# Attention with a gated second layer: which unit's outputs are turned by TensorE, in a newly searched order of steps

## The chip, the cores and the metric

The kernel runs on one core of one Trainium2 chip. The metric is the device time of one execution in microseconds (us). The engines are named as the profile names them: PE is TensorE, DVE is VectorE, ACT is ScalarE, POOL is GpSimd, SP is SyncE. PE, DVE and ACT compute here; POOL computes small things and issues DMA transfers; SP only issues them.

Executions of the kernel before spread from 169 to 187 us. A run is marked fast up to some 1.5% above the fastest of the same kernel (here up to 171.8 us), and slow above that, mostly with a slightly lower mean TensorE clock. In the rounds of the experiments 44 of its 76 executions were slow. The times run on without a gap at 172 us, so the mark is a convention. There is no other core that could disturb it. I compare fast with fast unless I say otherwise.

## The reference, cut to what matters

```python
# q, k, v: (4 batches, 8 heads, 768 positions, 64)
scores = q @ k.T / 8 - slope[h] * distance        # local window of 96 keys + 8 global keys
a = softmax(scores);  attn = a @ v                # (4, 8, 768, 64)
x = attn.transpose(0, 2, 1, 3).reshape(3072, 512)
h = x @ w_in                                      # (3072, 1024)
solu = h * softmax(h)
ln = (solu - mean) / sqrt(var + 1e-6) * g_ln
out = ln @ w_out                                  # (3072, 512), float32
```

## The kernel before

The work is cut into 12 units (4 batches x 3 stretches of 256 positions), each of two tiles of 128 rows in the second part. The kernel is a list of 662 steps, and the list *is* the schedule: each engine executes its own steps strictly in the order of the list, and waits where a step's input or buffer is not ready. A step that issues a DMA stands in the same list, on the engine that its letter names (S, A or P for SP, ACT or POOL).

```python
ORDER = """
...
M:6:0 o:D:1:0 o:A:1:1 Q:3:1 d:S:0:1 q:P:8:1 gk:2 q:P:10:0 cv:D:5 v:S:6:1 k:S:9:1 S:7:2 X:7:2
...
X:10:2 S:10:1 X:10:1 Q:5:0 O:4:0 A:6:1 E:6:1 o:D:4:0 U:6:1 dq:S:11 eq:D:11 v:P:9:1 cv:D:9 S:9:2
X:9:2 d:S:5:0 L:8 I:8 st:S:2 O:4:1 d:S:6:0 V:8 N:8 Z:P:5:0 S:11:3 S:11:2 X:11:3 Z:P:4:1 gv0:3
...
"""
    queues = {"S": nc.sync, "A": nc.scalar, "P": nc.gpsimd}
    def load_v(queue, u, j):                      # v:P:9:1 = half 1 of unit 9's v, issued by GpSimd
        ...
        queues[queue].dma_start(out=held["v32", u][:, :, j], in_=v[...])      # 256 KB
    def cast_v(engine, u):                        # cv:D:9 on VectorE, cv:A:9 on ScalarE
        t = held["v16", u] = attn.tile([P, H, 2, D], FP16, name="v16", bufs=NV)
        cast(engine, t, held.pop(("v32", u)))
    def pick_global_k(b):                         # gk:2, on GpSimd
        for m in range(2):
            nc.gpsimd.tensor_copy(out=z[rr, :, m * NG : m * NG + NG], in_=kT[rr, :, 0:NG])
    def ff_stats(engine, t):                      # Z:P:u:r: five 128x1 operations on GpSimd
        eng.tensor_scalar(out=w1, in0=s0, scalar1=s0, scalar2=1e-6, ...)
        ... (mean, w2, w3)
        eng.tensor_tensor(out=rs, in0=w3, in1=held["neghalf"], op=ALU.pow)
    def ff_turn(t, h=None):                       # t: turn by TensorE, into a small PSUM buffer
        lT = held["lT", t, h] = small([P, len(cs), P], FP16, "lT")
        for i, c in enumerate(cs):
            nc.tensor.transpose(out=lT[:, i], in_=held["un", t][:, ts(c, P)], ...)
    def ff_turn_dma(queue, t):                    # d: turn by a DMA transpose
        queues[queue].dma_start_transpose(out=held["uT", t, None], in_=held["un", t])
    def warm_up(n, i=0):                          # warm: dummy matmuls on zeros
        t = small([P, 512], FP32, "warm")
        ...
    with tc.manual_schedule():
        for step in ORDER.split():
            run(step)
```

The other letters that the text uses: `A`, `E`, `U`, `Q` are the first matmul of the second part (PE), its exponential (ACT), product (DVE) and square (ACT); `Z` the statistics of a tile (mean and inverse deviation, one column each); `O` the second matmul (PE), `o` its scaling, `st` the store; `S`, `X`, `M`, `L`, `I`, `V`, `N` are scores, exponential, mask, sums, reciprocal, values and norm of the attention; `gS` the scores of the global keys, which need `gk`; `tq` turns (transposes) a unit's q on PE, `dq` and `dk` turn by DMA. PSUM is the memory that PE writes its results to; its "small" buffers are two, its "big" ones three, and a step waits until its buffer is free.

The softmax here doesn't subtract the row's maximum and nothing guards it: scores larger than these inputs give would overflow.

## Time and profile before

| | before |
|---|---|
| time, three runs | 171.25 us median (170.24, 171.25, 177.0) |
| profiled execution | 170.78 us, span 169.0 us, mean clock 1.00 |
| busy share PE / ACT / DVE / POOL | 90% / 83% / 78% / 59% |

The profile sets each engine's busy time beside the span. It is easy to read the 59% of POOL as "room"; the result will turn on that. The prediction shows the stretches it used; three others matter for what follows. Columns: stretch, its length, busy us and instruction count of PE, weight loads, DVE, ACT and POOL, then clock (1.00 is full speed), DMA share and GB/s.

```profile
80.00:90.00 10.00, 8.78 (x92) 4.42 (x90) 9.12 (x13) 8.48 (x16) 9.03 (x17) 1.00 1.09 258
...
120.00:130.00 10.00, 10.00 (x110) 5.36 (x110) 8.91 (x16) 8.45 (x15) 7.51 (x15) 1.00 0.94 196
130.00:140.00 10.00, 10.00 (x122) 5.88 (x118) 6.42 (x8) 8.58 (x13) 3.25 (x10) 1.00 0.36 39
```

PE has a small gap near 80 us and none from 120 to 140, at full clock throughout; POOL is busy 9.03 of 10 us near 80. When POOL issued the two loads of interest, the timeline of POOL shows (start, length, engine, what):

```profile
76.15 0.55 POOL L157 DMA_DIRECT2D q<-in_q_dram  x1
76.69 1.09 POOL L320 COPY kgz<-kT 64x32 f16<-64x32 f16 x2
...
104.05 1.87 POOL L163 DMA_DIRECT2D v<-in_v_dram  x2
```

The first is the second half of unit 8's q, the next the pick of the global keys (`gk:2`), the last contains the second half of unit 9's v, which VectorE casts at 114.22 us: about 9 us after it was issued at some 105.0 (the second of the two in the 1.87 us).

### The profile page before, as it was taken

How to read it: one execution, taken by the hardware profiler on the slowest of the kernel's cores; microseconds unless marked ns; L12 is line 12 of the kernel's file. 1: busy time of each engine (PE TensorE's matmuls, PEld its weight loads, DVE VectorE, ACT ScalarE, POOL GpSimd, SP SyncE). 2: the span in 40 equal slices, each digit the busy share in tenths (PEclk: the TensorE clock that was granted, in tenths of full speed). 3: DMA queues.
4: the chain of work that ended last, by engine and by line, in shares of the span. 5: the costliest groups of instructions: out<-in, count | busy, mean ns of one | idle time of the engine just before them, and what ended most of it. 6: DMA issues, size and time to landing. Idle time of an engine off the chain costs nothing.

```text
span 169.0 us, 3944 instructions
## 1 busy us (share of the span) xinstructions
PE 151.6 (90%) x1487; PEld 81.6 (48%) x1487; DVE 132.0 (78%) x203; ACT 140.0 (83%) x218; POOL 100.3 (59%) x194
## 2 busy tenths in 40 slices
...
GB/s 147 329 349 259 238 238 243 200 376 363 372 258 276 194 170 203 144 245 235 251 292 169 203 312 228 136 215 272 275 77 248 42 2 190 124 186 122 132 181 124
DMA packets 59698, 36.43 MB, mean 215 GB/s; under 512 B 50592, under 2 KB 51104, under 8 KB 59680
## 3 DMA queue, kind: packets, MB, share of 16 engines
...
## 4 chain that ended last, share of the span: by engine, by line
PE 48%; ACT 18%; DMA 14%; POOL 10%; issue 6%; DVE 2%; SPq 1%; DVEq 0%; POOLq 0%; ACTq 0%
PE po L512 17%; PE ph L450 16%; DMA q<-in_q_dram 5%; ACT pt L338 4%; PE lb L398 4%; DMA v<-in_v_dram 4%; ACT e L462 3%; PE warm L230 3%; PE sc L329 2%; ACT sq L475 2%; DMA uT<-un 2%; DMA k<-in_k_dram 2%; PE pa L417 2%; ACT rlb L406 2%; POOL gw L588 2%
## 5 line engine op out<-in xcount | busy, mean ns | idle before, releaser
L512 PE MATMUL po<-gw,uT 128*128 128x512 f16 x192 | 44.8, 380 | 1.4 <-DMA uT<-un 1.1
L450 PE MATMUL ph<-w_in,xT 128*128 128x512 f16 x192 | 44.3, 379 | 1.1 <-DVE xT L435 0.8
L338 ACT ACTIVATE pt<-sc 128x896 f16<-128x896 f32 (+1 forms) x48 | 39.2, 873 | 2.0 <-PE sc L329 1.9
L467 DVE SCALAR_TENSOR_TENSOR un<-e,ph 128x1024 f16<-128x1024 f16 x24 | 29.0, 1218 | 6.4 <-ACT e L462 4.6
L462 ACT ACTIVATE e<-ph 128x1024 f16<-128x1024 f32 x24 | 24.5, 1021 | 7.9 <-PE ph L450 7.6
L450 PEld LDWEIGHTS <-xT 128*128 128x128 f16 x192 | 18.2, 98 | 22.5 <-DVE xT L435 1.5
L512 PEld LDWEIGHTS <-uT 128*128 128x128 f16 x192 | 17.7, 98 | 23.1 <-DMA uT<-un 2.4
L475 ACT ACTIVATE sq<-un 128x1024 f16<-128x1024 f16 x24 | 25.4, 1059 | 2.5 <-DVE un L467 2.0
L345 DVE TENSOR_TENSOR pt<-pt,mask 128x896 f16<-128x896 f16 (+1 forms) x48 | 26.3, 586 | 0.6 <-ACT pt L338 0.6
L488 POOL TENSOR_SCALAR w<-s,w 128x1 f32<-128x1 f32 x24 | 9.9, 414 | 17.7 <-ACT sq L475 15.9
L527 DVE TENSOR_SCALAR osb<-po,rs 128x512 f32<-128x512 f32 x17 | 12.7, 748 | 8.5 <-PE po L512 8.5
L329 PE MATMUL sc<-qT,kT 64*128 64x128 f16 (+2 forms) x256 | 16.6, 248 | 2.8 <-DVE kT L140 1.3
L435 DVE TENSOR_TENSOR xT<-pa,rlb 128x1024 f16<-128x1024 f32 x12 | 14.6, 1220 | 2.5 <-ACT rlb L407 1.8
L490 POOL TENSOR_TENSOR rs<-w,neghalf 128x1 f32<-128x1 f32 x24 | 14.8, 619 | 2.0
L483 POOL TENSOR_SCALAR w<-s 128x1 f32<-128x1 f32 x24 | 14.1, 586 | 2.5 <-ACT e L462 0.4
L140 DVE COPY qT<-qturned 128x1024 f16<-128x1024 f16 x9 | 11.0, 1220 | 5.3 <-PE qturned L301 5.3
L329 PEld LDWEIGHTS <-kT 64*128 64x128 f16 x256 | 9.2, 100 | 10.2 <-issue 6.2
L486 POOL TENSOR_SCALAR w<-mean,w 128x1 f32<-128x1 f32 x24 | 11.6, 483 | 2.4
L407 ACT ACTIVATE rlb<-rlb 128x1024 f32<-128x1024 f32 x12 | 12.7, 1058 | 0.4
L301 PE MATMUL qturned<-ident,q 128*128 128x128 f16 x72 | 6.6, 250 | 7.0 <-POOL hm L242 6.6
L406 ACT ACTIVATE rlb<-lb 128x1024 f32<-128x1024 f32 x12 | 12.3, 1025 | 0.7 <-PE lb L398 0.6
L417 PE MATMUL pa<-pt,v 128*64 128x128 f16 (+2 forms) x256 | 10.9, 232 | 0.0
...
## 6 DMA issues: line engine op xcount, KB each, us to landing
...
```

The costliest lines, as they stand in the source:

```text
L329: nc.tensor.matmul(out=sc[:, m, o : o + e - a], lhsT=held["kT", u - s + j // 2][r, g, ts(j % 2, P)], rhs=qT[r, g, a:e], start=True, stop=True,
L338: nc.scalar.activation(out=pt[:, :, 0:w], in_=held.pop(("sc", u, g))[:, :, 0:w], func=AF.Exp, scale=inv_sqrt_d)
L345: nc.vector.tensor_tensor(out=pt[:, :, 0:w], in0=pt[:, :, 0:w], in1=held["mask"][:, g, :, o : o + w], op=ALU.mult)
L406: nc.scalar.activation(out=rlb, in_=held.pop(("lb", u)), func=AF.Ln)
L417: nc.tensor.matmul(out=po[m * D : m * D + D, g, a:e], lhsT=held["v16", u - s + j // 2][:, 2 * g + m, j % 2], rhs=pt[:, m, o : o + e - a], ...
L435: nc.vector.tensor_tensor(out=xT.rearrange("p g (r i) -> p g r i", r=2), in0=held.pop(("pa", u)).rearrange("p g (i r) -> p g r i", r=2), i ...
L450: nc.tensor.matmul(out=held["ph", t][:, ts(fh, 512)], lhsT=held["xT", t[0]][:, j, ts(t[1], P)], rhs=held["w_in"][:, j, ts(fh, 512)], start ...
L462: nc.scalar.activation(out=held["e", t], in_=held["ph", t], func=AF.Exp, accum_out=s0)
L467: nc.vector.scalar_tensor_tensor(out=held["un", t], in0=held["e", t], scalar=1.0, in1=held["ph", t], op0=ALU.mult, op1=ALU.mult, accum_out=s1,
L475: nc.scalar.activation(out=sq, in_=held["un", t], func=AF.Square, accum_out=s2)
L490: eng.tensor_tensor(out=rs, in0=w3, in1=held["neghalf"], op=ALU.pow)
L512: nc.tensor.matmul(out=held["po", t], lhsT=held["uT", t, h][:, i, :], rhs=held["gw"][:, c, :], start=(c == 0), stop=(c == NFC - 1),)
```

## The change

The intent, as I read the diff: the output of the unit that is finished last, unit 9, is turned by TensorE in halves and stored in halves, so that the end no longer waits for a DMA transpose; unit 11, which had this, goes over to DMA transposes like all others. With it the whole order was searched anew. No function changes; only the list does. The end of it, and two places in the middle that will matter (cut):

```diff
@@ middle, near 65-85 us @@
-M:6:0 o:D:1:0 o:A:1:1 Q:3:1 d:S:0:1 q:P:8:1 gk:2 q:P:10:0 cv:D:5 v:S:6:1 k:S:9:1 S:7:2 X:7:2
+E:3:1 U:3:1 S:6:0 M:5:0 S:6:2 X:6:2 O:1:1 M:5:3 O:1:0 o:D:1:0 M:6:2 X:6:0 q:P:8:1 o:A:1:1 Q:3:1
...
+o:D:0:1 v:S:6:1 cv:D:6 k:S:10:0 S:7:0 X:7:0 cq:D:8 L:5 I:5 q:P:9:1 V:5 N:5 gk:2 gS:7 gv0:2
@@ middle, near 100-130 us @@
-X:10:2 S:10:1 X:10:1 Q:5:0 O:4:0 A:6:1 E:6:1 o:D:4:0 U:6:1 dq:S:11 eq:D:11 v:P:9:1 cv:D:9 S:9:2
-X:9:2 d:S:5:0 L:8 I:8 st:S:2 O:4:1 d:S:6:0 V:8 N:8 Z:P:5:0 S:11:3 S:11:2 X:11:3 Z:P:4:1 gv0:3
+cq:D:11 dq:S:9 d:S:4:1 O:3:1 o:D:3:1 eq:D:9 M:8:1 cv:D:8 S:10:2 dk:S:11 Q:4:1 Z:P:4:1 S:10:1
...
+X:11:3 M:11:3 M:10:1 st:S:2 Z:P:5:0 Z:P:6:0 v:P:9:1 O:5:0 o:A:5:0 M:10:3 v:P:10:0 gS:11 gX:11
+S:11:1 X:11:1 S:9:0 X:9:0 st:A:3 cv:A:9 S:11:0 X:11:0 d:S:6:0 O:6:0 A:8:0 E:8:0 U:8:0 M:11:2
@@ end @@
-st:A:11:1:1 d:S:9:0 O:9:0 o:A:9:0 d:S:9:1 st:S:10 O:9:1 o:D:9:1 st:S:9 warm:4:4 warm:5:1 warm:5:2
-warm:4:5
+o:D:10:1 st:A:10 o:A:9:0:1 st:A:9:0:1 t:9:1:0 o:D:9:0:0 st:S:9:0:0 t:9:1:1 e:D:9:1:0 e:A:9:1:1
+O:9:1:0 O:9:1:1 warm:4:4 o:A:9:1:1 st:S:9:1:1 warm:5:2 warm:5:1 o:A:9:1:0 st:A:9:1:0 warm:4:5
```

Three shifts can be seen in this diff already. The pick of the global keys, `gk:2`, stood right behind `q:P:8:1` and now has two more loads of q ahead of it. The load `v:P:9:1` stood ahead of the statistics `Z:P:5:0`, `Z:P:4:1` and `Z:P:6:0`; now all three stand ahead of it, and its cast is on ScalarE, not VectorE. And the transpose `d:S:3:0` (not in the cut) stood just ahead of `dk:S:9` on SP and now stands behind it.

More of the change, by code (lines that the diff above doesn't have):

```diff
@@ L26 @@
 ORDER = """
-k:A:2:0 q:S:0:0 q:S:0:1 off:1 dist:1 mask:1:7 mask:1:1 mask:1:4 off:0 id zero cap q:A:1:0 dist:0
-mask:0:6 hm cq:A:0 mask:0:2 mask:0:0 mask:0:5 mask:0:7 mask:1:3 fill tq:0 eq:D:0 k:S:0:0 k:S:0:1
-ck:P:0 v:A:0:0 mask:0:4 mask:1:6 mask:1:2 mask:0:1 mask:1:0 mask:0:3 tk:0 ek:D:0 S:0:2 q:S:1:1
-cq:P:1 X:0:2 S:0:0 tq:1 gk:0 X:0:0 S:0:3 gS:0 gb gX:0 S:0:1 X:0:1 X:0:3 k:S:1:0 k:S:1:1 ck:P:1
-k:S:2:1 q:S:2:0 q:S:2:1 cq:P:2 eq:D:1 gS:1 gX:1 q:A:3:0 mask:1:5 tk:1 ek:A:1 tq:2 eq:D:2 k:S:4:0
-selV M:0:3 v:S:0:1 ck:A:2 cv:P:0 wi:0 S:1:2 X:1:2 k:S:4:1 q:S:4:0 ck:D:4 S:1:1 X:1:1 k:S:3:0
@@ L33 @@
-k:S:3:1 ck:A:3 tk:2 ek:D:2 q:S:4:1 q:S:3:1 S:1:0 S:1:3 X:1:3 X:1:0 M:0:0 M:0:2 gv0:0 gv:0 M:1:1
-k:S:5:0 k:S:5:1 S:2:1 X:2:1 tk:4 ek:A:4 cq:D:4 M:1:2 tk:3 M:0:1 M:1:3 M:1:0 ek:D:3 gk:1 S:2:3
-v:A:1:0 X:2:3 v:S:2:0 v:S:1:1 wi:2 S:2:2 warm:5:3 g:S cq:D:3 X:2:2 S:2:0 X:2:0 M:2:2 cv:P:1
-k:P:6:0 L:0 I:0 tq:4 eq:D:4 tq:3 L:1 I:1 gS:2 ck:D:5 q:S:5:0 q:S:5:1 V:0 eq:D:3 S:3:0 X:3:0 gX:2
-N:0 tk:5 ek:D:5 k:P:8:0 k:P:8:1 k:P:7:0 S:4:3 S:3:3 X:4:3 X:3:3 M:3:0 V:1 N:1 M:2:0 S:3:1 X:3:1
-S:4:1 X:4:1 M:2:1 S:3:2 gS:4 gS:3 X:3:2 M:3:2 S:4:2 gX:4 X:4:2 M:3:1 M:4:2 M:2:3 M:4:1 M:4:3
@@ L39 @@
-q:P:7:0 q:S:7:1 k:S:6:1 v:S:2:1 q:S:6:0 q:P:6:1 k:P:7:1 S:4:0 X:4:0 gX:3 A:0:0 E:0:0 A:1:0 E:1:0
-wo:S:0 sc:P:0 L:2 I:2 A:1:1 E:1:1 wo:A:4 A:0:1 E:0:1 U:0:0 Q:0:0 ck:D:6 U:1:0 Z:P:0:0 cq:D:5 M:3:3
-L:3 I:3 M:4:0 cv:D:2 tq:5 V:2 wo:S:2 sc:P:3 wo:S:6 L:4 I:4 v:S:3:0 v:S:3:1 U:1:1 U:0:1 N:2 eq:D:5
-v:S:4:0 ck:D:7 cq:D:6 ck:D:8 tk:6 ek:D:6 k:P:9:0 q:P:8:0 cv:D:3 gv0:1 A:2:1 sc:A:7 E:2:1 sc:A:6
-v:S:4:1 pr:6 U:2:1 A:2:0 E:2:0 U:2:0 warm:12 gv:1 Q:1:1 sc:A:1 sc:P:2 pr:7 sc:A:5 pr:5 S:5:0 X:5:0
-v:S:5:0 S:5:3 Z:P:1:1 tq:6 eq:D:6 V:3 N:3 v:S:6:0 d:S:0:0 cq:D:7 v:P:9:0 q:P:9:0 cv:D:4 sc:A:4
@@ L45 @@
-d:S:1:0 S:5:2 X:5:3 X:5:2 gS:5 gX:5 mean cm ce:0 ce:1 ce:2 S:6:3 S:5:1 X:6:3 X:5:1 V:4 N:4 S:6:1
-ce:3 ce:4 sm:5 sm:6 sm:7 Q:1:0 Q:0:1 Z:P:0:1 Z:P:1:0 tq:7 eq:D:7 d:S:1:1 M:6:3 A:3:0 E:3:0 U:3:0
-X:6:1 A:4:0 E:4:0 U:4:0 M:5:0 M:5:1 dk:S:7 ek:D:7 O:0:0 Q:2:1 Z:P:2:1 o:A:0:0 A:3:1 S:6:0 S:6:2
-O:1:1 M:6:1 Q:4:0 E:3:1 U:3:1 v:S:5:1 X:6:2 M:6:2 X:6:0 M:5:2 M:5:3 dk:S:8 ek:D:8 O:1:0 k:P:10:0
-M:6:0 o:D:1:0 o:A:1:1 Q:3:1 d:S:0:1 q:P:8:1 gk:2 q:P:10:0 cv:D:5 v:S:6:1 k:S:9:1 S:7:2 X:7:2
-v:S:7:0 S:7:3 X:7:3 S:7:1 X:7:1 k:S:10:1 O:0:1 o:D:0:1 d:S:2:0 q:P:9:1 q:P:10:1 cv:D:6 gv0:2
@@ L51 @@
-v:P:7:1 S:7:0 X:7:0 ck:D:9 d:S:2:1 d:S:3:0 cq:D:8 dk:S:9 M:7:1 L:5 I:5 V:5 N:5 k:P:11:0 gS:6 gS:7
-A:4:1 gX:7 gX:6 tq:8 eq:D:8 Q:2:0 q:S:11:0 E:4:1 U:4:1 Q:3:0 v:P:8:0 gv:2 A:5:1 E:5:1 U:5:1 L:6
-I:6 S:8:0 X:8:0 ck:A:10 M:7:2 O:2:0 dk:S:10 Z:P:2:0 M:7:3 o:D:2:0 V:6 S:8:1 X:8:1 cq:A:10 dq:S:10
-S:8:3 X:8:3 O:2:1 N:6 A:6:0 E:6:0 ek:D:9 o:A:2:1 gS:8 M:7:0 L:7 I:7 cv:D:7 V:7 cq:D:9 U:6:0 S:8:2
-Q:6:0 gX:8 X:8:2 v:P:11:0 M:8:0 v:P:11:1 cv:D:11 O:3:0 N:7 k:S:11:1 d:S:3:1 ek:A:10 Z:P:4:0
-Z:P:3:1 Z:P:3:0 M:8:3 ck:D:11 eq:D:10 A:5:0 E:5:0 q:S:11:1 cq:D:11 U:5:0 Q:5:1 o:D:3:0 A:7:0 E:7:0
@@ L57 @@
-U:7:0 st:S:0 gk:3 d:S:4:0 st:S:1 A:7:1 E:7:1 U:7:1 M:8:2 gS:10 S:10:3 X:10:3 O:3:1 o:D:3:1 dq:S:9
-M:8:1 eq:D:9 gX:10 Q:4:1 dk:S:11 d:S:4:1 ek:D:11 Z:P:5:1 S:10:0 X:10:0 v:P:8:1 cv:D:8 S:10:2
-X:10:2 S:10:1 X:10:1 Q:5:0 O:4:0 A:6:1 E:6:1 o:D:4:0 U:6:1 dq:S:11 eq:D:11 v:P:9:1 cv:D:9 S:9:2
-X:9:2 d:S:5:0 L:8 I:8 st:S:2 O:4:1 d:S:6:0 V:8 N:8 Z:P:5:0 S:11:3 S:11:2 X:11:3 Z:P:4:1 gv0:3
-o:D:4:1 v:P:10:0 X:11:2 Z:P:6:0 O:5:0 o:D:5:0 d:S:5:1 st:S:3 gS:11 Q:6:1 M:10:1 v:S:10:1 S:11:1
-X:11:1 gX:11 S:9:0 S:11:0 X:9:0 X:11:0 st:S:4 M:11:3 M:10:2 M:10:3 M:10:0 O:6:0 Q:7:0 A:8:0 M:9:2
@@ L63 @@
-E:8:0 M:11:2 M:9:0 o:D:6:0 U:8:0 S:9:3 d:S:7:0 M:11:0 M:11:1 L:10 I:10 Q:8:0 O:5:1 o:D:5:1 st:S:5
-cv:D:10 d:S:6:1 A:8:1 gv:3 X:9:3 E:8:1 U:8:1 O:7:0 Z:P:7:0 gS:9 gX:9 S:9:1 X:9:1 M:9:3 M:9:1
-d:S:7:1 L:11 I:11 V:10 V:11 o:D:7:0 N:10 Q:7:1 d:S:8:1 N:11 L:9 I:9 V:9 N:9 Q:8:1 d:S:8:0 A:10:0
-E:10:0 U:10:0 Z:P:6:1 Q:10:0 A:11:0 O:6:1 o:D:6:1 E:11:0 U:11:0 A:9:0 E:9:0 Z:P:8:1 Z:P:7:1
-Z:P:8:0 O:7:1 Q:11:0 Z:P:11:0 Z:P:10:0 A:10:1 U:9:0 o:D:7:1 Q:9:0 t:11:0:1 e:D:11:0:1 O:8:0
-o:D:8:0 O:8:1 o:D:8:1 t:11:0:0 e:D:11:0:0 E:10:1 U:10:1 A:11:1 E:11:1 U:11:1 O:11:0:0 O:11:0:1
@@ L69 @@
-o:D:11:0:0 st:S:6 st:S:7 d:S:10:0 Q:10:1 o:A:11:0:1 st:A:11:0:1 Z:P:9:0 O:10:0 o:A:10:0
-st:A:11:0:0 Z:P:10:1 t:11:1:0 e:D:11:1:0 Q:11:1 A:9:1 st:S:8 t:11:1:1 e:D:11:1:1 O:11:1:0 O:11:1:1
-E:9:1 U:9:1 Z:P:11:1 o:D:11:1:1 o:A:11:1:0 st:A:11:1:0 d:S:10:1 O:10:1 o:D:10:1 Q:9:1 Z:P:9:1
-st:A:11:1:1 d:S:9:0 O:9:0 o:A:9:0 d:S:9:1 st:S:10 O:9:1 o:D:9:1 st:S:9 warm:4:4 warm:5:1 warm:5:2
-warm:4:5
+off:1 off:0 cap id hm dist:1 mask:1:3 mask:1:4 q:A:1:0 dist:0 mask:1:0 q:S:0:0 q:S:0:1 cq:A:0
+mask:0:3 tq:0 k:S:0:0 k:S:0:1 ck:D:0 q:S:1:1 cq:P:1 eq:D:0 tk:0 ek:D:0 S:0:3 S:0:2 mask:0:6
@@ new lines @@
+mask:0:2 mask:1:7 mask:0:1 v:A:0:0 mask:0:7 fill mask:1:6 mask:0:4 mask:1:2 X:0:3 M:0:3 gb zero
+selV gk:0 gS:0 k:S:1:0 k:S:2:0 k:S:2:1 q:S:2:0 k:S:1:1 ck:P:1 tq:1 X:0:2 mask:1:1 mask:1:5 ck:P:2
+mask:0:0 S:0:0 X:0:0 gX:0 S:0:1 X:0:1 eq:D:1 gS:1 gX:1 q:S:2:1 cq:P:2 q:A:3:0 tk:1 ek:A:1 v:S:0:1
+mask:0:5 k:S:4:0 k:S:4:1 tq:2 eq:D:2 cv:P:0 M:0:2 ck:D:4 S:1:1 S:1:2 X:1:1 M:1:1 S:1:0 X:1:2 gv0:0
+gv:0 tk:2 M:0:0 ek:D:2 wi:0 M:1:2 X:1:0 M:1:0 k:S:3:0 q:S:4:0 k:S:3:1 ck:A:3 q:S:4:1 cq:D:4
+q:S:3:1 k:S:5:0 k:S:5:1 M:0:1 S:1:3 X:1:3 M:1:3 tk:4 ek:A:4 v:S:1:0 v:S:1:1 S:2:2 X:2:2 S:2:3
@@ new lines @@
+X:2:3 v:S:2:0 g:S S:2:1 X:2:1 tk:3 ek:D:3 gk:1 warm:5:3 cq:D:3 M:2:2 S:2:0 L:0 X:2:0 tq:4 eq:D:4
+I:0 wi:2 L:1 I:1 ck:D:5 tq:3 eq:D:3 gS:2 gX:2 V:0 N:0 S:3:0 X:3:0 S:4:3 tk:5 ek:D:5 gS:3 S:4:1
+X:4:3 M:4:3 q:S:5:0 v:S:2:1 q:S:5:1 X:4:1 S:3:3 X:3:3 cv:P:1 V:1 k:P:8:0 k:P:8:1 k:P:7:0 k:P:6:0
+k:P:7:1 N:1 M:2:0 k:S:6:1 S:3:1 X:3:1 q:S:6:0 q:P:7:0 q:P:6:1 S:4:2 gS:4 X:4:2 M:3:3 M:3:1 M:2:3
+M:4:1 S:4:0 X:4:0 S:3:2 M:4:0 gX:4 X:3:2 M:2:1 A:0:0 E:0:0 U:0:0 M:3:2 A:1:0 E:1:0 U:1:0 wo:S:0
+sc:P:0 wo:A:4 L:2 I:2 A:1:1 E:1:1 gX:3 M:3:0 A:0:1 E:0:1 cq:D:5 M:4:2 cv:D:2 Q:0:0 Z:P:0:0 L:3 I:3
@@ new lines @@
+tq:5 V:2 v:S:3:0 wo:S:6 v:S:3:1 U:1:1 sc:A:1 wo:S:2 v:S:4:0 ck:D:6 tk:6 L:4 I:4 k:P:9:0 U:0:1 N:2
+A:2:1 q:P:8:0 eq:D:5 sc:A:6 E:2:1 cq:D:6 ck:D:8 ck:D:7 cv:D:3 ek:D:6 pr:6 A:2:0 E:2:0 U:2:1
+warm:12 U:2:0 q:S:7:1 gv0:1 sc:P:2 gv:1 sc:P:3 Q:1:1 sc:A:7 tq:6 eq:D:6 sc:A:5 S:5:0 X:5:0 sc:A:4
+S:5:3 X:5:3 v:S:4:1 V:3 N:3 pr:7 S:5:2 X:5:2 gS:5 pr:5 gX:5 Z:P:1:1 cv:D:4 v:P:9:0 mean cm cq:D:7
+ce:0 ce:1 S:6:3 X:6:3 S:5:1 X:5:1 V:4 N:4 S:6:1 X:6:1 q:P:9:0 ce:2 ce:3 ce:4 tq:7 eq:D:7 Q:2:1
+M:5:1 sm:5 sm:6 sm:7 Z:P:2:1 v:S:5:0 v:S:6:0 A:3:0 E:3:0 Q:1:0 U:3:0 A:4:0 E:4:0 Q:0:1 d:S:0:0
@@ new lines @@
+O:0:0 o:A:0:0 Z:P:1:0 d:S:1:0 U:4:0 Q:4:0 d:S:1:1 M:5:2 dk:S:7 ek:D:7 v:S:5:1 cv:D:5 Z:P:0:1 A:3:1
+E:3:1 U:3:1 S:6:0 M:5:0 S:6:2 X:6:2 O:1:1 M:5:3 O:1:0 o:D:1:0 M:6:2 X:6:0 q:P:8:1 o:A:1:1 Q:3:1
+q:P:10:0 M:6:1 dk:S:8 ek:D:8 M:6:0 S:7:1 X:7:1 M:7:1 M:6:3 S:7:3 X:7:3 S:7:2 X:7:2 d:S:0:1 O:0:1
+o:D:0:1 v:S:6:1 cv:D:6 k:S:10:0 S:7:0 X:7:0 cq:D:8 L:5 I:5 q:P:9:1 V:5 N:5 gk:2 gS:7 gv0:2
+q:S:10:1 gS:6 gX:6 gX:7 A:4:1 M:7:2 gv:2 Q:2:0 M:7:0 k:S:9:1 ck:D:9 Z:P:2:0 E:4:1 U:4:1 d:S:2:0
+cq:D:9 k:S:10:1 tq:8 eq:A:8 v:S:7:0 d:S:2:1 k:P:11:0 A:5:1 E:5:1 U:5:1 L:6 I:6 O:2:0 o:D:2:0
@@ new lines @@
+v:P:7:1 V:6 N:6 k:S:11:1 q:S:11:0 q:S:11:1 ck:A:10 S:8:1 S:8:0 X:8:0 X:8:1 Q:3:0 gS:8 gX:8
+v:P:11:0 v:P:11:1 O:2:1 o:A:2:1 M:7:3 A:6:0 E:6:0 dk:S:9 L:7 I:7 S:8:3 X:8:3 d:S:3:0 O:3:0 cv:D:7
+ek:D:9 v:P:8:0 gk:3 cq:D:10 V:7 Z:P:4:0 U:6:0 dk:S:10 M:8:0 ek:A:10 Q:6:0 ck:D:11 cv:D:11 N:7
+S:8:2 X:8:2 A:5:0 E:5:0 dq:S:10 eq:D:10 M:8:2 d:S:3:1 st:S:0 d:S:4:0 M:8:3 Q:5:1 U:5:0 Z:P:3:0
+o:D:3:0 A:7:0 E:7:0 v:P:8:1 U:7:0 A:7:1 E:7:1 U:7:1 S:10:3 Z:P:3:1 Z:P:5:1 X:10:3 gS:10 gX:10
+cq:D:11 dq:S:9 d:S:4:1 O:3:1 o:D:3:1 eq:D:9 M:8:1 cv:D:8 S:10:2 dk:S:11 Q:4:1 Z:P:4:1 S:10:1
```

10 lines of the change are left out of this document (added).

## The prediction

> **What bounds the kernel now.** The order string is the whole change, so I first asked which engine is full, and when. The page gives PE 151.6, ACT 140.0 and DVE 132.0 us busy of 169.0: three engines near their limit. I then read the busy time by stretches (columns: stretch, its length, then busy us and instruction count for PE, weight loads, DVE, ACT, POOL; clock; DMA share; GB/s).
>
> ```profile
> 0.00:17.00 17.00, 6.41 (x61) 4.59 (x62) 8.64 (x20) 12.84 (x25) 10.73 (x29) 1.00 0.87 271
> 35.00:60.00 25.00, 24.32 (x268) 13.41 (x268) 24.13 (x37) 23.82 (x38) 9.87 (x20) 1.00 1.08 299
> 100.00:120.00 20.00, 19.49 (x184) 9.74 (x183) 18.31 (x28) 19.36 (x31) 13.81 (x23) 1.00 0.97 221
> 140.00:157.00 17.00, 17.00 (x92) 8.05 (x90) 9.47 (x17) 10.48 (x20) 9.98 (x30) 1.00 0.60 155
> 157.00:169.00 12.00, 9.86 (x44) 3.89 (x42) 2.65 (x5) 2.31 (x4) 1.43 (x4) 1.00 0.53 153
> ```
>
> The reader is to see four regimes: a start in which PE mostly waits for loads, a middle in which PE, DVE and ACT are all about full, a stretch up to 157 us that PE alone fills, and an end with waits. The chain of waits agrees: from 106.45 us to 157.86 us it is PE without a break. Its last pieces (start, length, what):
>
> ```profile
> 155.56 2.30 PE po L512 x11
> 157.86 4.13 DMA uT<-un
> 162.00 0.05 issue
> 162.04 1.91 PE po L512 x8
> 163.99 0.05 issue
> 164.04 0.05 DVEq L527
> 164.13 0.76 DVE osb L527
> 164.90 0.04 issue
> 164.94 3.18 PE warm L230 x14
> ```
>
> The last tile (unit 9, tile 1) is turned by a DMA transpose; PE waits for it, multiplies, DVE scales, and the last thing to end is not the store but 14 dummy matmuls. They need the buffer that the scaling frees, so they start 0.04 us after it and end at 168.12; 0.9 us of closing work make 169.0. The list of waits gives the exposed part of the DMA transposes and two other waits that I use below:
>
> ```profile
> PE po L512 <- DMA uT<-un: 1.1, 2, 0.8
> ACT osbh L529 <- DVE osbh L527: 2.4, 2, 1.7
> DVE q L140 <- DMA q<-in_q_dram: 0.9, 1, 0.9
> ```
>
> Of the 4.13 us of the transpose PE stands still for 0.8 us on tile 0 and 0.3 on tile 1; the rest lies under other tiles' matmuls. Last, the timeline of the start:
>
> ```profile
> 0.82 0.66 ACTq L157 DMA_DIRECT2D k<-in_k_dram  x1
> 6.65 1.04 PE L301 MATMUL qturned<-ident,q 128*128 128x128 f16 x8 [6.65 <-POOL hm L242]
> 9.65 1.03 PE L301 MATMUL kturned<-ident,k 128*128 128x128 f16 x8 [1.97 <-POOL k L142]
> 12.00 0.77 PE L329 MATMUL sc<-qT,kT 64*128 64x224 f16 x8 [1.32 <-DVE kT L140]
> ```
>
> The first scores start at 12.00, behind two loads, two casts, two turns and two copies.
>
> **What the Trainium skill says.** "TensorE: Matmul & The Clock Gate", Part 4: PE-mode transpose, says that a TensorE transpose lands in PSUM and needs a copy after it, and gives some 275 ns for one in a kernel. Here one shows as 219 ns and four in a row take 0.22 us of the chain; their copy takes 0.42 us on DVE. "PSUM — Partial Sum Buffer", PSUM bank collisions raise a hardware error, says that ScalarE and VectorE must not touch one bank and quadrant at once, reads included. The trace is consistent: ACT's half of an output waits until DVE's half is done (the 2.4 us over two cases above), so halves on two engines run one after the other. "DMA: Bandwidth & Descriptors", Issuing engines are not separate DMA queues, says that loads from all issuers share the 16 engines: an extra load on ACT's queue delays SP's. The trace only fits it: the DMA share is 0.87 over the first 17 us.
>
> **The change part by part.** The numbers of matmuls and transposes stay: before, unit 11's two tiles were turned on PE in four halves and unit 9's, the last, by DMA; now 9's by PE and 11's by DMA.
>
> Start. One load of unit 2's k (256 KB at 0.82 us) leaves the front. Up to 8.45 us the page moves about 2.0 MB (147 and 329 GB/s in slices of 4.225 us), so 0.26 MB less at 330 GB/s brings unit 0's q and k about 0.8 us earlier. The cast of k goes from POOL (1.04 us) to DVE (0.69). DVE does it before copying q, so: k lands at 7.7, cast to 8.45, q copied (1.23) to 9.7, k copied to 10.9, first scores at about 11.0 instead of 12.00. ACT then has 0.4 us more to do before the first reciprocal (at 28.28 us now): four masks for one, +1.5, less the cast of unit 2's k (1.05) that goes to POOL. I credit 0.7 us of the 1.0.
>
> Middle. At 80.5 us DVE waited 0.9 us for a load of q that POOL issued at 76.15, behind another load (1.41 us of issue). That load moves to SP, so the wait should go. ACT gives unit 10's q cast (1.06) to DVE and takes unit 8's q copy (1.05), a draw. Other engines are nearly full there, so I credit 0.5 of the 0.9.
>
> Stretch of PE. Its work is conserved, only ordered otherwise: one second-layer tile (unit 7, tile 1) moves ahead of the last attention unit. ACT takes on two casts of v (2.1 us) and three more scalings (3 x 0.69), and puts off one squaring (1.25): +2.9 us up to the last reciprocal. It idles 3.0 us in 120 to 140 now, so this should just fit; it gives nothing.
>
> Tail. The last attention unit ends now at 133.64 and would end at 133.64 + 1.73 (the moved tile) = 135.37, less the 1.2 us gained earlier. From there I followed the orders of PE, ACT and DVE with the durations of the page. PE has 15 tiles of 1.73 us and four half turns of 0.22 = 26.8 us. Three places stop it, all from the two small PSUM buffers: the second half turn of tile 0 waits for DVE to scale unit 10's tile (about 0.7 us), the turns of tile 1 wait for the two halves of tile 0's output, which go one after the other (1.1 us), and the first product of tile 1 waits for its copy (0.2 us). So the last matmul ends about 28.8 us after the attention; before it was 163.94 - 133.64 = 30.3 with one tile more (28.6 in like terms). The turn on PE thus saves the 1.1 us of DMA waits and pays it back in buffer waits. Then both halves of the last output are scaled on ACT, 2 x 0.47 and some gaps = 1.2 us after the last matmul, where DVE needed 0.95.
>
> The end. The last store shrinks from 512 to two of 128 KB (3.4 and 2.9 us to landing), but the 14 dummy matmuls still start when the last scaling ends and still take 3.2 us, about what issue plus landing takes (0.35 + 2.9). So the smaller store gives nothing that can be seen.
>
> Sum: 135.37 + 28.8 + 1.2 + 3.2 + 0.9 = 169.5 without the early gains, 169.5 - 1.2 = 168.3 with them, against 169.0: about 0.7 us less. From 170.78 (the run profiled) and 171.25 (median of three) this makes 170.1 and 170.5; I say 170.2.
>
> **Rivals.** First: the tail gains fully. If ACT and DVE free the small buffers sooner than I worked out, the 2.0 us of buffer waits mostly vanish and the time is near 168.5. For it: DVE and ACT have room after 140 us (9.5 and 10.5 of 17). Against: the waits come from the order on the two buffers, not from load. Second: ACT becomes the bound between 107 and 135 us. For it: it is at 19.36 of 20 in 100 to 120 and gets 2.9 us more; then the last reciprocals come late, and the time is 171 to 172. Against: the 3.0 us idle right after. Third: the start is hidden. ACT works through 16 masks and the exponentials without large gaps, so earlier scores would only let it wait elsewhere; then only 0.5 us of early gain stays, and the time is near 171. Fourth: a late load or transpose in the new SP order (unit 10's v now goes behind two transposes that wait for buffers). It would stop PE for a microsecond or so; by my count there are 2.4 us of slack.
>
> **Range and chances.** The early gain is 1.2 with about 0.8 either way, the tail 0 with about 1.2 either way, and the median of three runs carries half a microsecond of its own (170.24 and 171.25 for the same kernel). I take 168.3 to 171.9. Two per cent is 3.4 us; for that both tail and start would have to go right by more than I can find, and to lose as much ACT would have to be a bound throughout. Faster 0.10, same 0.86, slower 0.04.
>
> **What would show it.** Start: first scores near 11.0 us, first reciprocal near 27.6. Middle: no wait of DVE for q near 80 us. Tail: PE's last real matmul about 28.8 us after the last attention matmuls; waits of half turns for DVE or ACT in place of waits for a DMA; the chain ending again in dummy matmuls. I am wrong if PE runs through to its last matmul without those waits, if ACT shows no idle time in 107 to 135 with PE waiting for a reciprocal, or if PE waits for v or a transpose.

## The result, and the profile after

| | before | after |
|---|---|---|
| time | 173.24 us median of 4 (170.24, 171.25 fast; 175.23, 177.0 slow) | 183.56 us median of 4 (181.95, 182.71, 184.42 fast; 184.94 slow) |
| ratio of fast runs | | 1.0719, 95% interval 1.0528 to 1.0911 |
| profiled span | 169.0 us | 183.2 us |
| mean clock | 1.00 | 0.963 to 0.981 |

Ratios here are the mean time of one kernel's fast runs over that of the other's fast runs of the same rounds, so not quite the ratio of the medians: (181.95 + 182.71 + 184.42) / 3 = 183.03 over (170.24 + 171.25) / 2 = 170.75. The change makes the kernel 7% slower. I had predicted 170.2.

The only profile of the changed kernel fell in its one run marked slow (184.94, clock 0.963). It differs from its fast runs by little: the two half-clock stretches shown below last 6.83 us each, and 1 - 0.5 x 13.66 / 183.2 = 0.963. Clocks of 0.972 and 0.981 answer to 10.2 and 6.8 us at half clock. So the fast runs have half-clock stretches as well, only less of them, and the fast profiles of E1 and E4 below, whose orders are almost this one, show the same kinds of waits.

First the page's slices, 40 of 4.58 us each: the busy tenths of PE and the clock that PE got.

```profile
PE   0246789799999999976999999999279999999887
...
PEclk9999999999999999995699999999965999999999
```

Where before nearly every slice after the start was at 9, there are two holes: the 18th and 19th slice (78 to 87 us) and the 29th (128 to 133). With the first and after the second, the clock is near half for two slices. The stretches in numbers (columns as before):

```profile
0.00:17.00 17.00, 5.06 (x48) 3.42 (x48) 9.81 (x22) 11.26 (x22) 6.68 (x25) 1.00 0.72 225
...
80.00:90.00 10.00, 7.24 (x60) 3.57 (x57) 5.18 (x9) 5.90 (x10) 8.80 (x17) 0.66 0.80 232
...
120.00:130.00 10.00, 9.63 (x92) 4.63 (x85) 5.08 (x8) 5.59 (x9) 7.23 (x8) 1.00 0.94 193
130.00:140.00 10.00, 5.82 (x39) 2.60 (x39) 3.82 (x7) 7.95 (x11) 5.29 (x13) 0.72 0.56 131
```

From 130 to 140 us PE executed 39 matmul instructions where it had executed 122. In 80 to 90 all of PE, DVE and ACT fell; only POOL stayed at its level (8.80 against 9.03). That is the shape of one engine holding up the three others. The list of PE's waits (what waited for what: us in total, times, longest):

```profile
PE lb L388 <- ACT pt L337: 3.6, 1, 3.6
...
PE gs L357 <- POOL kgz L319: 2.8, 1, 2.8
...
PE lT L495 <- DVE osbh L526: 0.9, 1, 0.9
PE lT L495 <- DVE osb L526: 0.7, 1, 0.7
```

The first two are new and make the holes. The last two are the buffer waits of the half turns that the prediction had named (0.9 and 0.7 us). The timeline of PE at the holes (in brackets the idle time before and what ended it):

```profile
83.98 0.43 PE L357 MATMUL gs<-qT,kgz 128*32 128x256 f16 x8 [2.77 <-POOL kgz L319]
84.35 3.59 PE L449 MATMUL ph<-w_in,xT 128*128 128x512 f16 x8
...
133.27 0.39 PE L388 MATMUL lb<-pg,hm 64*128 64x256 f16 x4 [3.64 <-ACT pt L337]
133.60 1.03 PE L397 MATMUL lb<-pt,ones 128*64 128x96 f16 x24
135.54 3.57 PE L449 MATMUL ph<-w_in,xT 128*128 128x512 f16 x8 [0.91 <-DVE un L466]
```

Eight matmuls of 512 columns take 3.59 and 3.57 us here; elsewhere in this trace the same eight take 1.89 (at 125.75 us). So each hole costs the wait and then some 1.7 us more for this group alone, and more for the next (nine matmuls at 139.33 in 3.03 us).

To put the time to its places, I matched every PE step of one order with the same step of the other and took the difference in start. The changed kernel is 2.2 us late by 79 us, all of it from the start (first scores at 12.79 instead of 12.00, first matmul of the second part at 39.43 instead of 37.19). It is 6.1 late after the hole near 81 us. Then it holds that level until 129.6, and is 13.7 late after the second hole, once one second-layer tile (1.73 us) that moved ahead of the last attention unit is taken off: the values of unit 9 end at 149.22 instead of 133.71, so 15.5 - 1.7. So 2.2 + 3.9 + 7.6 = 13.7 us of a difference in span of 14.2 (one trace each; that the 2.2 us at the start is a lasting loss is tested in H3). The tail gives the other half microsecond.

Why did the two things come late? Both stand in the queue of POOL (the timeline of POOL, parts):

```profile
77.93 2.83 POOL L487 TENSOR_SCALAR w<-s,w 128x1 f32<-128x1 f32 x1
...
81.35 2.09 POOL L156 DMA_DIRECT2D q<-in_q_dram  x3
83.44 0.49 POOL L319 COPY kgz<-kT 64x32 f16<-64x32 f16 x2
...
122.90 2.34 POOL L487 TENSOR_SCALAR w<-s,w 128x1 f32<-128x1 f32 x1
125.32 0.56 POOL L489 TENSOR_TENSOR rs<-w,neghalf 128x1 f32<-128x1 f32 x1
125.83 1.85 POOL L162 DMA_DIRECT2D v<-in_v_dram  x2
```

The load of unit 8's q is issued at 81.35 instead of 76.15 and the global keys are copied at 83.44 instead of 76.69. The load of unit 9's v is issued at 125.83 instead of some 105. In front of both stand chains of statistics, five operations on one column each, of which some take 2.3 to 2.8 us instead of the usual 0.29. Ahead of q they are the chains of the same three tiles as in the old order. There POOL was through with them at 74.8 us, here at 81.4: it came to them 2.95 us later, and they took 12.4 us instead of 8.8. Between the loads of unit 8's and unit 9's v stand five chains and, in the old order, none. They fill POOL from 106.81 to 125.88 us almost without a gap. The second hole stands on the chain of waits (start, length, what), and so does the end:

```profile
125.83 5.45 DMA v<-in_v_dram
...
132.32 0.90 ACT pt L337
...
135.54 3.57 PE ph L449 x8
...
176.30 1.87 PE po L511 x8
178.16 0.02 issue
178.19 0.85 ACT osbh L528 x2
...
179.08 3.18 PE warm L229 x14
```

ACT came to the cast of v in its queue at 125.8, waited 5.57 us for the load, and everything behind the cast waited with it, among it the exponential of unit 11's scores (`X:11:0`), which frees the PSUM buffer that PE needs for the sums of unit 10. The end is as predicted, with dummy matmuls as the last piece and no DMA transpose in it.

### The profile page after: what moved, and what is told of

It is laid out like the page before. It is cut to its first block, busy times and chain, and to the rows that moved or that the text cites. A ratio compares the mean times of both kernels' runs of the same rounds, so it can differ in the third digit from the quotient of the medians.

```text
span 183.2 us, 3947 instructions
## 1 busy us (share of the span) xinstructions
PE 157.6 (86%) x1487; PEld 84.3 (46%) x1487; DVE 127.9 (70%) x196; ACT 143.9 (79%) x225; POOL 101.2 (55%) x192
## 5 line engine op out<-in xcount | busy, mean ns | idle before, releaser
L449 PE MATMUL ph<-w_in,xT 128*128 128x512 f16 x192 | 47.6, 403 | 1.1 <-DVE un L466 0.9
L466 DVE SCALAR_TENSOR_TENSOR un<-e,ph 128x1024 f16<-128x1024 f16 x24 | 28.9, 1216 | 12.3 <-ACT e L461 12.1
L449 PEld LDWEIGHTS <-xT 128*128 128x128 f16 x192 | 19.2, 102 | 24.7 <-issue 5.2
L487 POOL TENSOR_SCALAR w<-s,w 128x1 f32<-128x1 f32 x24 | 13.1, 545 | 18.3 <-ACT sq L474 16.6
L526 DVE TENSOR_SCALAR osb<-po,rs 128x512 f32<-128x512 f32 x15 | 11.3, 755 | 11.4 <-PE po L511 6.8
L489 POOL TENSOR_TENSOR rs<-w,neghalf 128x1 f32<-128x1 f32 x24 | 17.5, 729 | 2.0
L328 PE MATMUL sc<-qT,kT 64*128 64x128 f16 (+2 forms) x256 | 15.9, 252 | 2.7 <-DVE kT L139 1.7
L485 POOL TENSOR_SCALAR w<-mean,w 128x1 f32<-128x1 f32 x24 | 14.7, 611 | 2.4
L300 PE MATMUL qturned<-ident,q 128*128 128x128 f16 x72 | 7.3, 261 | 6.9 <-ACT q L137 6.0
L139 DVE COPY qT<-qturned 128x1024 f16<-128x1024 f16 x8 | 9.7, 1218 | 4.5 <-PE qturned L300 4.5
L319 POOL COPY kgz<-kT 64x32 f16<-64x32 f16 x8 | 3.0, 373 | 15.1 <-DVE kT L139 14.8
```

Source lines behind the costliest of these rows:

```text
L328: nc.tensor.matmul(out=sc[:, m, o : o + e - a], lhsT=held["kT", u - s + j // 2][r, g, ts(j % 2, P)], rhs=qT[r, g, a:e], start=True, stop=True,
L449: nc.tensor.matmul(out=held["ph", t][:, ts(fh, 512)], lhsT=held["xT", t[0]][:, j, ts(t[1], P)], rhs=held["w_in"][:, j, ts(fh, 512)], start ...
L466: nc.vector.scalar_tensor_tensor(out=held["un", t], in0=held["e", t], scalar=1.0, in1=held["ph", t], op0=ALU.mult, op1=ALU.mult, accum_out=s1,
L485: eng.tensor_scalar(out=w2, in0=mean, scalar1=mean, scalar2=w1, op0=ALU.mult, op1=ALU.subtract)
L487: eng.tensor_scalar(out=w3, in0=s2, scalar1=1.0 / D_FF, scalar2=w2, op0=ALU.mult, op1=ALU.subtract)
```

## The experiments

Each edit is to the list of steps, and each kernel gave a correct result. E1 to E4 shared a chip and the runs of the kernel before; so did the next four, the next four, and the last three. Times of one group are compared with the runs of before of that group.

My theory after the comparison: two loads and one copy stand too late in POOL's queue, and the pauses that they make bring the half clock. The rivals: the new tail, the new start, or an overload of ACT. The profiles of E2, E3, G1, G2 and J1 to J4 fell in runs marked slow.

**E1: unit 9's v issued early** (changed kernel; from behind five chains of statistics to just after its neighbour).

```
- E:7:0 v:P:8:1 U:7:0 ... Z:P:5:0 Z:P:6:0 v:P:9:1 O:5:0
+ E:7:0 v:P:8:1 v:P:9:1 U:7:0 ... Z:P:5:0 Z:P:6:0 O:5:0
```

> The changed kernel with one load moved: the second half of unit 9's v is issued by GpSimd right behind the second half of unit 8's v, as in the kernel before, no longer behind three tiles' statistics. Theory A (the time is lost where GpSimd's queue holds loads and copies back; the profile of after puts some 7.5 us of the 14.2 lost at this load): about 175.5 us, and no wait of PE over 1 us near 130 us. Theory B (the loss is the half clock that follows any long pause, and another pause takes its place): over 180. Theory C (ScalarE is overloaded in that stretch by the casts and scalings it was given): 181 to 183, ScalarE full there.

Measured: 179.37 us median of 4 (178.19 to 179.79), clock 0.98 to 0.99. The wait of PE at 129 us is gone, the one near 80 us is still there (2.7 us). But a wait that the changed kernel did not have is there instead, at the second matmul of unit 3 (list of PE's waits):

```profile
PE po L511 <- DMA uT<-un: 3.3, 1, 3.3
```

So the load accounts for about 4 us (fast runs 179.2 against 183.0, on another chip), less than I expected, because a third thing was late too and had been hidden by the slower pace.

**E2: unit 8's q and the global keys early** (changed kernel; ahead of all three chains, so further forward than the kernel before had them).

```
- sm:7 Z:P:2:1 ... q:P:8:1 ... gk:2 gS:7
+ sm:7 q:P:8:1 gk:2 Z:P:2:1 ... gS:7
```

> The changed kernel with two steps moved: the second half of unit 8's q and the copy of the third batch's global keys come before the three statistics chains on GpSimd. Theory A: the wait of PE of 2.8 us near 81 us and the half clock behind it go, about 3.9 us less: 179.5 us. If GpSimd is not the cause there but the late start is: no change, 183.

Measured: 184.37 us median (182.72 to 185.68). A miss: no gain at all. The wait near 81 us fell from 2.8 to 1.2 us, but PE then waited 4.0 us for the transpose of unit 3 and 5.2 us at unit 10's sums. The time won at one late item was handed to the next late items, which do not get earlier when PE does.

**E3: both moves** (E1 and E2 in one kernel).

```
+ sm:7 q:P:8:1 gk:2 Z:P:2:1 ... v:P:8:1 v:P:9:1 ...
```

> Both moves. Theory A: the gains add, 183.5 - 7.5 - 3.9 = about 172 us, clock 1.00 throughout; what is left over the kernel before is the start, some 2.2 us late. Theories B and C: 178 or more.

Measured: 178.95 us median (fast 176.28 and 178.06, slow 179.85 and 182.89). A miss against 172. The timeline of PE has the remaining hole:

```profile
100.47 3.59 PE L511 MATMUL po<-gw,uT 128*128 128x512 f16 x8 [4.88 <-DMA uT<-un]
```

It is the transpose `d:S:3:0`. SP issued it at 87.8 us in this run; in the kernel before, at about 76. In the new order it stands behind `dk:S:9` in SP's queue, and that one waits for VectorE's cast of unit 9's k. The landing took longer than the usual 4 us as well (87.8 + 1.68 us of issue to 100.4), with the DMA engines full in this stretch.

**E4: dummy matmuls ahead of the two holes** (changed kernel), to keep the clock up and so to part the wait from the half clock.

```
+ gk:2 warm:12:7 gS:7
+ o:A:5:1 warm:16:8 L:10
```

> The changed kernel with dummy matmuls in its two pauses of PE: 12 before the first global scores of the third batch, 16 before the row sums of unit 10. The waits themselves stay. It parts the pause from the half clock after it. From the trace of after: the half clock costs about 1 us at the first and 3 us at the second, so if the clock follows from the pause: clock 1.00, about 179.5 us. If the clock falls for another reason: 183, clock 0.97.

Measured: 191.78 us median (190.22 to 194.41), worse as a whole. At the first hole it did what it was for (timeline of PE):

```profile
78.86 2.76 PE L230 MATMUL warm<-zeros 128*128 128x512 f16 x12
...
81.93 1.90 PE L450 MATMUL ph<-w_in,xT 128*128 128x512 f16 x8
```

The dummies fill the stop, the clock stays full until a later wait (99.98 us), and the next eight matmuls take 1.90 us, not 3.59. From the end of unit 5's values to the start of unit 2's second matmul PE takes 9.82 us here and 9.36 in E1, whose stop of the same length brought no half clock, against 10.98 in the changed kernel. So the half clock costs 1.2 to 1.6 us of the first hole, net of other small waits. At the second hole it failed: the dummies need a small PSUM buffer, which the blocked ACT was holding, so they waited 6.66 us themselves and then ran 5.65 us on PE's path, the first 4.2 of them at half clock. What the half clock costs there is left with the 3.6 against 1.9 us of the trace.

**G1: the old body with the new tail.** The kernel before up to the last norm of unit 9, then the changed kernel's list: the intent of the change without the new search.

```
  ORDER = before, up to and with N:9
  + after, behind N:9, less Q:6:1 d:S:8:1 (done earlier in the old order),
  +   led by Z:P:7:1 O:7:1 o:D:7:1 Z:P:8:0 st:A:7 d:S:8:0 (not yet done there)
```

> The order of the kernel before up to the normalising of the last attention unit (unit 9), then the order of the changed kernel: the stated intent of the change without the new search of the rest. Theory A (the intent is neutral as the prediction's sum for the tail says, 28.8 us from the last attention matmul to the last real one; the whole loss is in the order of the body): within 1% of before, fast against fast, 169 to 172 us. Theory D (the new tail itself costs): 175 or more.

Measured: 172.85 us median of 20, 10 of them fast (169.95 to 172.44); ratio of fast runs 1.0056 (1.0015 to 1.0097), beside 23 runs of before, 11 fast. The intent alone is half a per cent slower, about 1 us, in the direction of the prediction's sum without early gains (169.5 against 169.0).

**G2: the new body with the old tail**, the counterpart.

> The other graft: the changed order up to the same point, then the order of before, unit 11 turned by TensorE and unit 9 by DMA. Theory A: still 181 to 184 us, since the body loses the time. Theory D: near 175.

Measured: 186.58 us median (182.48, the one fast run, to 191.11), with waits of 2.7 us for the global keys, 3.1 for unit 3's transpose and 4.8 at unit 10's sums. With G1 this puts the loss into the body and clears the tail.

**H2: three moves** (E3, and the transpose of unit 3 ahead of `dk:S:9`, where the kernel before had it).

```
- d:S:2:1 k:P:11:0 ... dk:S:9 L:7 I:7 S:8:3 X:8:3 d:S:3:0 O:3:0
+ d:S:2:1 d:S:3:0 k:P:11:0 ... dk:S:9 L:7 I:7 S:8:3 X:8:3 O:3:0
```

> The kernel with both earlier moves, and the DMA transpose of unit 3's first tile issued by SP directly behind unit 2's, ahead of two loads and of the transpose of unit 9's k that waits for VectorE's cast. In the trace with two moves PE waits 4.9 us for this transpose, which SP issued at 87.8 us, in the kernel before at about 76. If SP's in-order queue is the cause: that wait goes, with the half clock behind it, 179 - 4 to 6 = about 174 us. If the transpose is slow because the DMA engines are full: the wait stays, 178 to 180.

Measured: fast runs 172.27, 172.33, 172.41, one slow of 184.28; ratio of fast runs 1.0122 (1.0057 to 1.0187). No PE wait over 1.3 us is left after the start, and the mean clock of the profiled run is 1.00. Moving four steps of 662 takes the ratio from 1.0719 to 1.0122, so about five sixths of the loss. All the casts and scalings that the change gave to ACT are still there, so an overload of ACT was not the cause.

**H3: the old start as well** (before up to the second reciprocal, `I:1`, then H2).

> The three moves, and the order of before for the start (up to the second unit's reciprocal). If the new start costs the 1.1 to 1.5 us by which the traces are late at 33 us: about 172.5 us. If the start differs only by chance of the loads: as with the three moves.

Measured: 173.05 us median (172.30 to 174.34); ratio 1.0171 (1.0081 to 1.0262). Not better than H2. In the kept profiles the first matmul of the second part comes at 37.1 to 39.4 us with the new start (eight traces) and at 35.6 to 37.6 with the old one (nine), so the new start is some 2 us later there. But giving the old one back did not make the kernel faster: in the profiles H3 is 1.6 us ahead of H2 at this matmul and 1.4 us behind it at the end of the attention.

**J4: the late load alone, in the kernel before.** The reverse of E1: the three statistics are moved ahead of the load of unit 9's v.

```
- eq:D:11 v:P:9:1 cv:D:9 ... Z:P:5:0 ... Z:P:4:1 ... Z:P:6:0
+ eq:D:11 Z:P:5:0 Z:P:4:1 Z:P:6:0 v:P:9:1 cv:D:9 ...
```

> The reverse of the first experiment: the kernel before, with the three statistics chains (units 5, 4 and 6) moved ahead of the load of the second half of unit 9's v on GpSimd, as in the changed kernel; the cast stays on VectorE. If that order is enough to cause the loss: the load goes out at 118 to 120 us rather than 105, VectorE's queue stands at the cast until about 125, and the time rises by 5 to 9 us to 175 to 179, with clock under 1. If the loss needs the other changes of the search too: within 1% of before.

Measured: 183.17 us median; the one fast run 178.79, against a mean of 170.0 for the four fast runs of before of the group. PE's wait at unit 11's global scores:

```profile
PE gs L358 <- DVE osb L527: 7.7, 1, 7.7
```

VectorE stood 7.90 us at the cast. The fast run lies at the upper end of what I expected, and shows that the mechanism is enough: one load put behind three short chains costs the good kernel some 9 us (the medians, 183.17 against 174.41, say the same). With one fast run the size is rough, and the profile, of the slowest run, has another stop of 3.3 us near 82 us.

**J1 and J2: without the closing dummies.** The 18 dummy matmuls at the end are taken out of the kernel before (J1) and of G1 (J2), because the chains of both end in them.

```
- warm:4:4 warm:5:1 warm:5:2 warm:4:5
```

> The kernel before without the 18 dummy matmuls at its very end. The prediction held that these end the program (168.12 us in the trace of before, while the last store has landed by about 167.4). If so: 0.4 to 0.7 us less than before, fast against fast, a ratio of 0.996 to 0.998, and the chain of waits ends in a DMA. If the store sets the end anyway: the same as before. If the dummies serve the end in a way that the trace does not show: slower.

> The graft of old body and new tail, without the 18 dummies. Its last stores are of 128 KB and landed in 1.9 us where before's 512 KB took some 2.5. If the dummies hid that: 0.9 us less than the graft (1.0056), so level with before, a ratio of 0.999 to 1.002. If not: 1.005.

Measured: J1 175.56 us median of 6, one fast run of 169.63; before in the group 174.41 median of 11, its fast runs 169.11 to 171.40. J2 171.98 median of 6, fast runs 169.02, 169.07 and 171.19, ratio 0.9985 (0.9857 to 1.0112). Inconclusive: whether the dummies set the end can't be told with so few fast runs. J2 is level with before.

**J3: unit 8's q and the global keys early in the kernel before** (without dummies). In a slow profile of J1, PE waits 3.4 us at the turn of unit 8's q near 84 us, and a half-clock stretch follows; I wanted to see whether this makes the slow runs.

```
- sm:7 Q:1:0 ... d:S:0:1 q:P:8:1 gk:2 q:P:10:0
+ sm:7 q:P:8:1 gk:2 Q:1:0 ... d:S:0:1 q:P:10:0
```

> A try to beat both: the kernel before without the dummies, and with the second half of unit 8's q and the copy of the third batch's global keys ahead of the three statistics chains on GpSimd. About half of before's runs are slow with a clock under 1, and a slow run of the graft shows waits of PE of 1.2 and 2.0 us at just these steps, near 80 us. If GpSimd's queue causes the slow runs: fewer than one in four slow, a median about 169.5; fast against fast 0.993 to 0.998. If the slow runs come from elsewhere: as many slow ones as before.

Measured: 173.04 us median of 6, one fast (169.38), five slow (172.43 to 176.34). A miss: that wait is gone, others of 1.0 to 1.4 us come later, and slow runs are as many.

The last three runs change the issuing engine instead of the place on POOL.

**K1 and K2: the load of unit 8's q issued by SP**, in the kernel before (K1) and in G1 (K2).

```
- d:S:0:1 q:P:8:1 gk:2
+ q:S:8:1 d:S:0:1 gk:2
```

> The kernel before with one load handed over: the second half of unit 8's q is issued by SyncE, just ahead of the transpose of unit 0's second tile, and no longer by GpSimd behind the statistics. If the slow half of the runs of the kernel before comes from that load leaving late behind statistics whose length varies, slow runs become rare (at most 1 of 6, against about half), fast runs stay at 169 to 171 us, and no wait of TensorE of more than 1.5 us is left at the turn of unit 8's q near 80 us. If the slow runs come from something else (the DMA engines being full), about half of the runs stay at 172 us and more.

> The old body with the new tail, and the same load handed to SyncE. With the theory of the late GpSimd load: nearly all runs at 170 to 172 us, so a median near 171 against 172.85 without it; ratio of fast runs 1.00 to 1.01. With the rival (full DMA engines): slow runs as many as before, about half.

Measured: K1 172.0 us median of 14, 5 fast; ratio 1.0004 (0.9951 to 1.0057). K2 171.88 of 22, 9 fast; ratio 0.9993 (0.9949 to 1.0037). Before in the group: 172.41 of 35, 16 fast. Slow runs did not become rare, so this part of the expectation is missed: the late load of q makes one wait of the slow runs, but is not what makes runs slow. (The worst of the slow runs were 176.7 and 179.1 us, against 187.3 of before, in fewer runs.)

**K3: the three moves with both late loads issued by SP.**

```
- q:P:8:1 gk:2 Z:P:2:1 ... v:P:8:1 v:P:9:1 ...      (of H2)
+ gk:2 Z:P:2:1 ... q:S:8:1 d:S:0:1 ... v:S:9:1 dq:S:9 ...
```

> The changed kernel with the transpose of unit 3's first tile moved as in the three moves, and with both late loads (half of unit 8's q, half of unit 9's v) issued by SyncE instead of GpSimd. If what matters is only that they no longer stand behind the statistics of GpSimd, this is 171 to 173.5 us like the three moves (172.4), with no wait of TensorE over 1.5 us between 35 and 150 us. If a load issued by SyncE is itself delayed behind transposes that wait for buffers, a wait of 2 us or more is seen at the second layer of unit 3 or the last attention units, and the time is 175 to 180.

Measured: 171.91 us median, all four fast (171.71 to 172.25); ratio 1.0107 (1.0044 to 1.0170). The page's slices of PE and clock:

```profile
PE   0363769789999999998999988999999999999877
...
PEclk9999999999999999999999999999999999999999
```

The two holes of the changed kernel are gone, with the loads on another engine (issued at 68.8 and 99.8 us); the copy of the global keys is early on POOL, as in E2. The DMA engines had the same bytes to move. What matters is that the loads are issued in time, not on which place of POOL's queue. No kernel of this study is clearly faster than the one before.

## Why the prediction was wrong

**The tail: right.** The last real matmul ends 28.9 us after the last attention unit (176.30 + 1.87 - 149.22); the prediction says 28.8. The buffer waits that it named were 0.7 us for the scaling of unit 10 and 0.9 of its 1.1 for the halves. The chain ends in dummy matmuls. From the end of the attention to the end of the span it is 34.0 us against 35.3 with one tile (1.73) more, so 0.4 us slower in like terms, and G1 measures 0.6% of some 170, about 1 us. "The turn on PE thus saves the 1.1 us of DMA waits and pays it back in buffer waits" holds.

**"Start": wrong, and small.** The credited 0.7 us was not there; first scores came at 12.79, not 11.0. In five other profiles with the new start they did come at 10.5 to 11.2 us, but this lead was lost before the first matmul of the second part (H3); why stays open. H3 shows that the order of the start is not worth a measurable gain either way.

**"Middle": this step failed.** The prediction says of the load of q at 80.5 us: "That load moves to SP, so the wait should go." That misreads the list: the load that POOL issued at 76.15 us is `q:P:8:1`, the second half of unit 8's q, and it stays on POOL; the load of q that goes to SP is the second half of unit 10's. The step also says nothing of the copy of the global keys, which stays on POOL too. The new order brings the two 5.2 and 6.75 us later in the pair of traces. In place of the 0.5 us credited, the trace has a wait of 2.8 us and a half-clock stretch: 3.9 us of loss. E1 and G2, which have the same order there, show the same wait (2.7 us each).

**"Stretch of PE": this step failed, and is the largest.** It says: "Its work is conserved, only ordered otherwise", and "it gives nothing". The work was conserved; what was not was the lead of a load over its use. Unit 9's v had some 9 us between issue and cast and had none after, which cost 7.6 us with the half clock that followed. E1 takes this wait away, and J4 puts the same kind of wait into the kernel before by one swap. My count was of ACT's busy time (19.36 of 20, +2.9 us, 3.0 idle). That rival, an ACT too full, is not what happened: ACT did not run out of time, it stood still for 5.57 us with a cast at the head of its queue.

**The fourth rival was the right kind, on the wrong queue.** I looked for late loads on SP (unit 10's v, 2.4 us of slack), and not on POOL, whose busy times I had printed and not used. A transpose that went late on SP was there as well, unit 3's, and showed only when the other two holes were mended (E2, E3). H2 and K3 show the three together: 1.0719 falls to 1.0122 and 1.0107. The rest, about 1%, is in part the tail (G1, 0.6%); the other half per cent is within the intervals. It also hangs on the marks: runs of 172.1 to 172.4 us count as slow for the kernel before and as fast for H2 and K3. The medians of all runs are level (H2 172.37 against 172.1, K3 171.91 against 172.41).

**The clock: not considered.** The Trainium skill, "TensorE: Matmul & The Clock Gate", Part 1, says that PE's clock falls to half after an idle window of some 3.4 us and comes back after some 3.4 us of work. This case agrees in kind: the stops of 2.8 and 3.6 us both led to 6.83 us at half clock, so a sum of waits from a list is less than their cost. But the length of the stop does not decide alone: in the first hole the clock fell at 83.16 us, 1.9 us after PE's last matmul (80.83 + 0.39), and in E1 a stop of 2.73 us at the same step led to none. The traces show more. The clock changes on a fixed grid of 3.41 us: the two falls of the changed kernel, at 83.16 and 134.36 us, are 51.20 us apart, 15 steps, and in all kept traces the half-clock stretches that end before the program does last 3.41, 6.83 or 10.24 us. These are the busy times in the grid stretch before the first fall, and in the two that the stop of E1 touches:

```profile
79.75:83.16 3.41, 1.47 (x40) 1.05 (x34) 2.28 (x4) 2.61 (x3) 3.33 (x5) 1.00 1.17 279
...
78.31:81.73 3.42, 1.66 (x46) 1.25 (x40) 2.44 (x5) 2.80 (x4) 3.34 (x5) 1.00 1.13 254
81.73:85.14 3.41, 2.36 (x17) 0.92 (x17) 0.40 (x1) 1.89 (x5) 2.50 (x8) 1.00 0.83 293
```

PE was busy 43% of the first, and 49% and 69% of the other two, because the grid cuts the stop of E1 in two. Worked out in the same way over the kept traces with clock changes, the clock fell after every stretch with PE busy 40% or less, after none with 56% or more, and either way between. Once at half it stayed so after stretches of up to 80% and came back after those of 85% and more. So what a stop of 2 to 3 us costs depends in part on where it falls.

**Why statistics are slow on POOL** was argued and not tested. The Trainium skill, "Perfetto Trace Analysis", Optimizing Scalar/DVE Operations, says that GpSimd and VectorE share a read port of SBUF and that a two-port VectorE operation holds it exclusively. The long operations (1.9 to 2.8 us for one column) lie where VectorE works almost without gaps, mostly on fp16 tiles, which fits. It is not enough: in the changed kernel two thirds of the short ones lie so too. Spans on POOL are rough. The skill's "DMA: Bandwidth & Descriptors", SWDGE vs HWDGE vs iDMA, adds that DMAs issued by GpSimd meet the same lock while their descriptors are written, and that those issued by SP or ACT don't. K3 fits: with both loads on SP the two holes are gone. It does not show the lock itself, since the loads also stand in another queue.

**What stays open.** What makes about half of the runs of the kernel before slow (K1 and J3 each took a suspect away, and slow runs stayed). Of its 44 slow runs 39 show a mean clock below 1, of its 32 fast ones one. The values go in steps of about 0.01, which is what one half-clock stretch makes of such a run (estimate: 0.5 x 3.41 / 175 = 0.0097). So slow runs are likely those in which PE stopped long enough somewhere, but none of this kernel was profiled. How much of the second hole is the half clock (E4 parted the first alone). Whether the closing dummies set the end (J1, J2). Why single transposes and loads take up to 12 us to land while the DMA engines are full.

## What to carry to other kernels

When a whole order is searched anew, compare for each load the time from its issue to its first use, on each issuing queue, before adding up busy times: an engine that is busy 59% can still deliver late what three others stand waiting for, because its queue is in order. After mending one late item look again, since the next late items take over the wait that was won, and several must be mended at once before the time moves. And count a stop of TensorE of some 3 us at more than its length, for the half clock that often follows (1.2 to 1.6 us more at the first hole here).

## What the Trainium skill lacked or had wrong

- "Perfetto Trace Analysis" names the port that GpSimd and VectorE share, but neither it nor another page gives what this can cost an operation of one column: 128x1 operations on GpSimd of usually 0.29 us show as 2.34 and 2.83 us beside a VectorE busy 93% and more (cause argued, not tested).
- "TensorE: Matmul & The Clock Gate" asks for an idle window of about 3.4 us. In these traces the window need not be idle: the clock fell after windows in which PE was busy up to 43% in the changed kernel (a stop of 2.77 us), and up to 55% in others. In E1 a stop of 2.73 us, cut in two by the grid, was not enough.
- "DMA: Bandwidth & Descriptors" gives a bandwidth for DMA transposes, but not how long a single one takes to land beside full load traffic: 4.13 us in the quiet end of the kernel before, some 12 us near 90 us in E3.
- No page says how far the times of one program on one core can spread: 169 to 187 us for the kernel before, 44 of 76 runs over 172 us, at a mean clock of 0.96 to 1.00.
